# Retention followed by a GELU MLP on one core: block 5's first product by seven half-size products, some differences of g on GpSimd, masks one by one, loads in another order

## The chip, the cores and the metric

The kernel runs on one core of a Trainium2 chip. The metric is the device time of one execution in microseconds (us). Three runs of the kernel before gave 300.93 us as their median (300.79 to 301.58). The engines are called as in the profile: PE (matrix products, with PEld for the weight loads beside it), DVE (vector), ACT (scalar), POOL (GpSimd, which also issues most of the loads), SP (which issues the loads of v and the stores).

## What is computed

```python
scores = scale * q @ k.T                      # 8 batches, 8 heads, 576 positions, 64 per head
ret    = scores * Dmat                        # gamma[h] ** (row - col) where row >= col, else 0
x      = (ret @ v), heads side by side        # 4608 tokens x 512
h      = x @ w_in                             # 512 -> 2048, "first product"
g      = 0.5 * h * (1 + erf(h / sqrt(2)))     # GELU
out    = g @ w_out                            # 2048 -> 512, "second product"
```

Inputs and output are float32; the kernel works in bfloat16 with float32 sums.

## The kernel before

The retention is done in chunks of 128 positions with a running state, so that a chunk needs its own scores and the state of the chunk ahead of it. A unit is one chunk of one batch (the last chunk of 64 positions joins two batches); a group is the same chunk of two batches. There are 36 units in 22 groups. For each group q and k are loaded and turned (by PE for groups 0 to 7, `turn`, and by a DVE transpose from group 8 on, `turn_dve`), the scores are made (`scores`, tile `sc`), multiplied by a mask into `ret` (`masked`, on DVE), multiplied by the scaled values `vh` (`scaled_v`, DVE or POOL) and joined with the state (`inner`, `cross`, tile `o_ps`); `evacuate` scales the result into a tile of x on DVE. `state` makes the next state from k, v (tile `u_ps`).

Four units make a block of 512 tokens, and there are nine blocks, 0 to 8. The first product of a block is by default 16 steps of four 128x512 matmuls (`mlp1`, tile `hT`), each followed by a GELU on ACT into `g_all`. In the blocks of `FAST1` (6, 7, 8) it is Winograd's form of Strassen's method instead: the product is cut into 2x2 parts and seven half-size products do for eight (`mlp1_fast`, 4 runs of 7 steps, each step four 128x256 matmuls, tiles `ha` and `hb`). It needs sums of the parts of w_in, made once (`w_in_sums`), sums of the parts of x (`x_sum`, four for each block), three copies of `ha` out of PSUM in each run (`either`: DVE or ACT, whichever the planner sees free first) and three additions on DVE (`plus`). The steps run in the order 1, 2, 6, 5, 7, 4, 3. The second product is `mlp2` (tile `oT`) or, in the blocks of `FAST2` (1 to 8), the same seven-product form in two halves of 256 tokens (`mlp2_fast`, 7 steps of eight 128x256 matmuls, tiles `fa` and `fb`); each half needs four sums or differences of g (`g_sum`, 128x1024 bfloat16, both inputs in SBUF, called s1 to s4 here; the third overwrites a part of g itself).

The order of everything is decided while the program is built: a planner keeps an expected clock for each engine (`T`), appends the next step whose inputs it expects to be ready, and gives idle DVE time to side jobs (`side_jobs`, chosen by a priority). On the chip each engine then runs its own list in that order and waits on semaphores alone. An engine that has nothing ahead in its list starts an instruction as soon as the semaphores allow, whatever clock the planner had in mind. Loads by POOL stand in its list in the order of `ORDER`, extended by `reload`; at most eight of them are under way. The eight PSUM banks are shared by all of this.

Of the kernel before, what the change touches and what calls it, by code (L numbers as in the profile page):

```python
# [17 lines left out]
def kernel(  # L18
# [47 lines left out]
    FAST1 = (6, 7, 8)  # L66
# [3 lines left out]
    N_LD = 4  # L70
    N_QKT = 4
    N_KN = 4
    VH_POOL = 20
    N_VH = 6
    N_XB = 4
    ALLOW = 0
    AHEAD = 14
    RATE = 3.8
    HOT = 7.5
    SLACK, SB, PER_G, PER_B, TURN0 = 1.6, 9.0, 8.0, 40.0, 3.0  # L80
# [5 lines left out]
    V_LEAD = 4  # L86
# [46 lines left out]
    near = ld_pool.tile([128, 2, HP, 128], FP32, tag="qk", bufs=N_LD, name="near")  # L133
# [77 lines left out]

    sw = [0.0]
# [16 lines left out]
    def qk_tile(name):  # L229
        return ld_pool.tile([128, 4 * H * D], BF16, tag="qk", bufs=N_LD, name=name)  # L230
# [4 lines left out]
    def tiles_of(i):  # L235
        g = groups[group_of[i]]
        if i not in loaded:
# [3 lines left out]
            else:  # L241
                n = group_of[i]
                if i != g[0]:
                    qk, kn = loaded[i - 1][0], loaded[i - 1][2]
                elif n not in BY_DVE:
                    qk = qk_tile("qk_ld").rearrange("p (a h j d) -> p a h j d", a=2, h=H, j=2)
                    kn = qk[:, 1]
                else:
                    qk = qk_tile("qkb_ld").rearrange("p (a f) -> p a f", a=2)
                    kn = ld_pool.tile([128, H, 2, D], BF16, tag="kn", bufs=N_KN, name="kn_ld") if len(g) > 1 else None  # L250
                loaded[i] = (qk, None if group_of[i] in BY_DVE else ld_pool.tile([128, H, D], BF16, tag="v", bufs=8, name="v_ld"), kn)
# [13 lines left out]
    def load(what, i):  # L265
# [43 lines left out]
        for jj in (j,) if j is not None else range(2):  # L309
# [3 lines left out]
            else:  # L313
# [7 lines left out]
    ORDER = ("wi0 io v0 k1 q1 v1 wi1 q2 k2 v2 wi2 k3 q3 v3 wi3 wi4 wi5 wi6 wi7 wo0 wo1 wo2 wo3 wo4 wo5 wo6 wo7 "  # L321
             "q4 k4 q5 k5 v4 v5 dq2 q6 k6 q7 k7 v6 v7 q8 k8 q9 k9 v8 v9 dq3 q10 k10 v10 dq4 q11 k11 q12 k12 n11 n12 dq0").split()
# [9 lines left out]

    def reload():
        if next_load[0] < N_G:
            g = groups[next_load[0]]
            if next_load[0] not in BY_DVE:
                ORDER.extend(f"{what}{i}" for what in "qkv" for i in g)
            else:
                ORDER.extend([f"{what}{i}" for what in "qk" for i in g] + [f"n{i}" for i in g if len(g) > 1])
            next_load[0] += 1  # L340

# [50 lines left out]
    def qkT_of(n):  # L392
        s = sg[n]
        if "qkT" not in s:
            if n < 4:
                s["qkT"] = ld_pool.tile([128, 2, HP, 128], BF16, tag="kn", bufs=N_KN, name="qkT")
            else:
                s["qkT"] = tr_pool.tile([128, 2, H, 128], BF16, tag="qkT", bufs=N_QKT, name="qkT")
# [88 lines left out]

    def masked(i):
        s = st[i]
        if i not in raw and any(x[3] is make_msk for x in later):  # L490
            finish_later()
        (got, done) = s.pop("sc")
        s["ret"] = []
        short = units[i][2] is None
        if short:
            r = ret_pool.tile([128, H, TAIL], BF16, tag="ret0", name="ret0")
        for e in range(2):
            b, t = got[e]
            sl = slice(64 * e, 64 * e + 64)
            if short and group_of[i] in BY_DVE:  # L500
                nc.vector.tensor_tensor(r[:, HP * e:HP * e + HP, :], t, msk2.to_broadcast([128, HP, TAIL]), op=ALU.mult)
            elif short:
                nc.vector.tensor_tensor(r[sl], t[sl], msk[sl, :, sl].to_broadcast([64, H, TAIL]), op=ALU.mult)
            else:
                r = ret_pool.tile([128, HP, 128], BF16, tag=f"ret{e}", name=f"ret{e}")
                by = near[:, e] if i in raw else (mskp if group_of[i] in BY_DVE else msk).to_broadcast([128, HP, 128])
                nc.vector.tensor_tensor(r, t, by, op=ALU.mult)  # L507
            s["R"] = on("dve", 0.42 if short and group_of[i] in BY_DVE else 0.66, done) + SEM
            release(b, s["R"])
            s["ret"].append(r)  # L510
# [209 lines left out]
    def g_sum(t, p, i):  # L720
# [7 lines left out]
        nc.vector.tensor_tensor(s[i], x, y, op=op)  # L728
        s["at" + i] = on("dve", 0.66, max(g_at[t, m, ts] for m in range(N_DF) for ts in (2 * p, 2 * p + 1))) + SEM
# [92 lines left out]
    def w_in_sums():  # L822
        def make(i, h):
            def go():
                if i not in ws:
                    ws[i] = qk_tile("ws" + i)[:, 0:HC * HF].rearrange("p (c f) -> p c f", c=HC)
# [9 lines left out]
    def x_sum(t, i):  # L836
# [4 lines left out]
        s[i] = ld_pool.tile([128, HC, HT], BF16, tag="v", bufs=8, name="x" + i)  # L841
# [5 lines left out]
    fast1 = {}  # L847

    def mlp1_fast(t, i, name):
# [31 lines left out]
        if name in "167":  # L881
            key = {"1": "t1", "6": "t2", "7": "t3"}[name]
            if key != "t2":
                f["tt"] = tr_pool.tile([128, 2, 2, HT], FP32, tag="qkT", bufs=N_QKT, name="tt")
            f[key] = f["tt"][:, key == "t2"]
# [17 lines left out]
    def fast1_ready(t, i, name):  # L903
        f, s = fast1.get((t, i), {}), xs.get(t, {})
        if ("f", t - 2, 0, "3") in waiting2 or nT < N_G or name == "7" and ("f", t - 2, 1, "4") in waiting2:
            return 1e9
        k_ = 2 * i + (name == "7")
        if name in "17" and t == FAST1[0] and k_ < N_QKT and nB <= groups[N_G - N_QKT + k_][-1]:
# [20 lines left out]
    for t in range(N_BLK):  # L929
# [13 lines left out]
        elif t == 0:  # L943
            runs2.append((t, [("2", t, ts, m, m + 2) for m in range(0, N_DF, 2) for ts in range(2)]))
            runs2.append((t, [("2", t, ts, m, m + 4) for ts in range(2, 4) for m in range(0, N_DF, 4)]))
# [36 lines left out]
    nA = nB = nT = nV = 0  # L982
# [7 lines left out]
    def xsum_ready(t, i):  # L990
        if t > FAST1[0] + 1 and ("h", t - 2, 3, {"1": "5", "2": "6", "4": "4", "3": "7"}[i]) in waiting2 or nV < N_U:
# [4 lines left out]
    for t in FAST2:  # L996
        for p in range(2):
# [5 lines left out]
    def sum_ready(t, p, i):  # L1003
        if i != "3" and t > FAST2[0] and not done_step(t - 1, p, {"1": "5", "2": "6", "4": "3"}[i]):
# [228 lines left out]
```

## Time and profile before

| what | value | from |
|---|---|---|
| median of three runs | 300.93 us | times |
| the profiled execution, whole | 300.81 us | times |
| its span, first to last instruction | 298.9 us | profile page |
| PE busy | 286.1 us, 96% | profile page |
| DVE busy | 226.7 us, 76% | profile page |
| ACT busy | 135.1 us, 45% | profile page |
| POOL busy | 152.9 us, 51%, nothing after 181.3 us | profile page |
| granted TensorE clock | 0.996 | times |

Busy counts any overlap once, and matmuls are pipelined: eight 128x256 matmuls that follow each other without a gap take 0.87 us, although one of them is shown with 273 ns. DVE instructions overlap in the same way at their ends: four masks in a row take 2.45 to 2.48 us, 0.60 us from one start to the next, although each is shown with about 0.68 us. Sums over the body are therefore made with the distance from start to start. In the trace block 1's first product begins at 51.7 us, that of block 5 at 175.3, block 6 at 208.8, block 7 at 230.7 and block 8 at 255.1 us.

### The profile page before, as it was taken

To read this page: it belongs to the slowest core of one execution; us is meant where nothing else is said; L and a number is where in the kernel's file an instruction comes from. 1 tells how busy PE (TensorE), PEld (TensorE's weight loads), DVE (VectorE), ACT (ScalarE), POOL (GpSimd) and SP (SyncE) were. 2 spreads that over 40 slices of the span, in tenths; PEclk is the share of its full clock that TensorE was granted. 3 is DMA by queue.
4 is the path that set the end of the run, shared out by engine and by line. 5 is a ranking of instruction groups with operands and counts; after the bars stand their busy time and mean duration, and the time that the engine had idled before them with its cause. 6 is when DMAs were issued, how large, how long until landed. Compare 5 with 4: busy or idle time off the path is not lost.

```text
span 298.9 us, 8793 instructions
## 1 busy us (share of the span) xinstructions
PE 286.1 (96%) x3689; PEld 213.8 (72%) x3718; DVE 226.7 (76%) x432; ACT 135.1 (45%) x262; POOL 152.9 (51%) x232
## 2 busy tenths in 40 slices
PE   7899997999999999999998999999999999999994
PEld 2478555888657656667665666666888888888883
DVE  5762059999999889317969489756998999898751
ACT  7656225744343343542542434433554554546421
POOL 8976797899896899996986842000000000000000
PEclk9999999999999999999999999999999999999998
DMA  9999999999999999999979570201001101111014
GB/s 143 166 186 204 182 187 179 214 163 113 155 141 197 189 201 125 155 162 159 139 126 174 83 188 2 72 2 37 35 2 72 71 2 70 44 28 72 35 55 124
DMA packets 112119, 34.79 MB, mean 116 GB/s; under 512 B 89808, under 2 KB 107728, under 8 KB 112080
## 3 DMA queue, kind: packets, MB, share of 16 engines
q0 software_dynamic: 78048, 17.71, 66.8%
q1 hardware_dynamic: 32992, 16.26, 20.2%
q8 instruction: 29, 0.48, 0.7%
q10 hardware_dynamic: 1040, 0.26, 0.4%
q14 instruction: 10, 0.08, 0.1%
HBM read 42.47 MB, written 9.44 MB: 174 GB/s over the span
## 4 chain that ended last, share of the span: by engine, by line
PE 62%; DMA 16%; POOL 16%; issue 3%; DVE 1%; ACT 0%; POOLq 0%; DVEq 0%; ACTq 0%
PE fa L760 17%; PE hT L656 14%; PE fb L760 13%; PE ha L865 7%; PE hb L865 5%; POOL qkb_ld L298 5%; DMA qkb_ld<-in_q_dram 3%; DMA qk_ld<-in_q_dram 3%; POOL kn_ld L305 3%; DMA kn_ld<-in_k_dram 3%; DMA w_out<-in_moe_w_out_dram 3%; POOL early L315 3%; DMA qk_ld<-in_k_dram 3%; PE sc L462 2%; POOL w_in L270 2%
## 5 line engine op out<-in xcount | busy, mean ns | idle before, releaser
L656 PE MATMUL hT<-x,w_in 128*128 128x512 bf16 (+2 forms) x521 | 92.6, 314 | 3.1 <-DVE x L636 1.0
L656 PEld LDWEIGHTS <-w_in 128*128 128x128 bf16 x544 | 49.1, 98 | 26.1 <-issue 3.2
L661 ACT ACTIVATE g_all<-hT 128x512 bf16<-128x512 f32 x64 | 38.2, 597 | 49.8 <-PE hT L656 47.6
L760 PEld LDWEIGHTS <-g_all 128*128 128x128 bf16 x512 | 49.6, 98 | 11.0 <-issue 0.2
L760 PEld LDWEIGHTS <-s 128*128 128x128 bf16 x384 | 37.4, 98 | 8.9 <-issue 0.2
L746 DVE TENSOR_TENSOR o_sb<-fb,t 128x256 f32<-128x256 f32 x48 | 19.9, 417 | 25.4 <-ACT t L375 12.9
L870 ACT ACTIVATE g_all<-tt 128x512 bf16<-128x512 f32 x36 | 22.6, 630 | 29.4 <-DVE tt L878 29.3
L298 POOL DMA_DIRECT2D qkb_ld<-in_k_dram x56 | 30.9, 587 | 6.5 <-DMA kn_ld<-in_k_dram 4.7
L760 PE MATMUL fa<-w_out,g_all 128*128 128x256 bf16 x256 | 33.1, 273 | 0.0
L305 POOL DMA_DIRECT2D kn_ld<-in_k_dram x44 | 30.4, 731 | 5.2 <-PE u_ps L557 2.3
L298 POOL DMA_DIRECT2D qkb_ld<-in_q_dram x56 | 31.3, 599 | 2.2 <-DMA qkb_ld<-in_k_dram 1.2
L507 DVE TENSOR_TENSOR ret<-sc,mskp 128x512 bf16<-128x512 f32 x44 | 27.2, 677 | 3.2 <-PE sc L462 3.1
L878 DVE TENSOR_TENSOR tt<-hb,tt 128x512 f32<-128x512 f32 x36 | 24.5, 687 | 5.2 <-ACT tt L375 2.9
L664 ACT ACTIVATE g_all<-hT 128x512 bf16<-128x512 f32 (+1 forms) x36 | 19.2, 550 | 14.2 <-PE hT L656 14.1
L375 ACT COPY t<-fa 128x256 f32<-128x256 f32 x35 | 13.0, 371 | 19.6 <-PE fa L760 19.6
L636 DVE TENSOR_TENSOR x<-o_ps,dqT 128x512 bf16<-128x512 f32 (+1 forms) x36 | 20.9, 619 | 0.8 <-PE o_ps L613 0.6
L865 PEld LDWEIGHTS <-ws 128*128 128x128 bf16 x192 | 18.8, 98 | 2.2
L516 POOL TENSOR_TENSOR vh<-v,dvp 128x512 bf16<-128x512 f32 x14 | 15.1, 1134 | 5.2 <-DMA v<-in_v_dram 5.2
L430 DVE STREAM_TRANSPOSE qkT<-qkb_ld 128x512 f32<-128x512 f32 (+1 forms) x28 | 17.4, 637 | 0.0
L760 PE MATMUL fb<-w_out,g_all 128*128 128x256 bf16 x128 | 16.6, 273 | 0.0
L760 PE MATMUL fb<-w_out,s 128*128 128x256 bf16 x128 | 16.4, 273 | 0.1
L760 PE MATMUL fa<-wt,g_all 128*128 128x256 bf16 x128 | 16.4, 273 | 0.0
(123 smaller groups left out, 445.2 us busy)
## 6 DMA issues: line engine op xcount, KB each, us to landing
out_dram<-o_sb SPq DMA_DIRECT2D x31, 256.0 KB, 2.8
v<-in_v_dram SPq DMA_DIRECT2D x50, 128.0 KB, 4.7
qkb_ld<-in_q_dram POOLq DMA_DIRECT2D x44, 64.0 KB, 3.6
qkb_ld<-in_k_dram POOLq DMA_DIRECT2D x44, 64.0 KB, 3.8
kn_ld<-in_k_dram POOLq DMA_DIRECT2D x44, 64.0 KB, 4.5
w_in<-in_moe_w_in_dram POOLq DMA_DIRECT2D x8, 256.0 KB, 7.1
w_out<-in_moe_w_out_dram POOLq DMA_DIRECT2D x8, 256.0 KB, 9.8
out_dram<-o_sb SPq DMA_DIRECT2D x8, 128.0 KB, 2.4
```

What stands on the lines that cost most here:

```text
L298: nc.gpsimd.dma_start(qk[p0:p0 + 32, "qk".index(what), 0:HP * per].rearrange("p (h x) -> p h x", h=HP), {"q": q, "k": k}[what][2 * bp + jj ...
L305: nc.gpsimd.dma_start(kn[64 * e:64 * e + 64, :, j], k[2 * bp + j, :, ci * C + e:ci * C + C:2, :].rearrange("h s d -> s h d"))
L507: nc.vector.tensor_tensor(r, t, by, op=ALU.mult)
L636: nc.vector.tensor_tensor(x[:, :, n * y:n * y + n], o, dqT[:, :, ci * C:ci * C + n], op=ALU.mult)
L656: nc.tensor.matmul(hT[:, m - m0, :], lhsT=w_in[:, cc, m * 128:m * 128 + 128], rhs=x_tiles[t][:, cc, lo:hi], start=(cc == 0), stop=(cc == N ...
L661: nc.scalar.activation(g_all[:, t % 2, :, m0, :], hT.rearrange("p n (a c) -> p (n a) c", a=2), AF.Gelu)
L664: nc.scalar.activation(g_of(t, 2 * lo // TOK)[:, m0:m0 + n, lo_:lo_ + hi - lo], hT, AF.Gelu)
L746: nc.vector.tensor_tensor(dst, src, f[key], op=ALU.add)
L760: nc.tensor.matmul(dst, lhsT=x[:, kk, :], rhs=y[:, kk, :], start=(name in "125" and kk == 0), stop=(kk == HK - 1), skip_group_check=True)
L865: nc.tensor.matmul(dst[:, m, :], lhsT=a[:, cc, c0:c0 + 128], rhs=y[:, cc, :], start=(name in "125" and m == 0 and cc == 0), stop=(cc == HC ...
L870: nc.scalar.activation(g_of(t, part)[:, m0:m0 + 2], src, AF.Gelu)
L878: nc.vector.tensor_tensor(f[key], f["b"][1], f[key], op=ALU.add)
```

## The change

- `FAST1` gets block 5: its 16 steps of `mlp1` become 4 runs of seven steps of `mlp1_fast`, which may now stand among the last attention groups (`fast1_ready`). One of the sums of w_in is written over w_in itself (`ws["3"]`), one gets its own tile.
- The second half of block 0's second product becomes the seven-product form as well, with its own four sums of g.
- Masks: `masked` only lists them, and `mask` makes one at a time as a side job.
- `g_sum` may be put on POOL when POOL is expected to be idle after 130 us of the planner's clock and the sum is not due at once. Of the 68 sums of the changed program 16 stand on POOL: s1 to s4 of the second half of blocks 4, 5 and 7, s1 to s3 of the second half of block 6, s1 of the second half of block 8. The other 52 stand on DVE (64 before).
- The loads: `ORDER` is another permutation, and from group 9 on a group's loads are listed only when the group whose buffer they take has been turned; the buffers of loads, turned tiles and values are split or reduced (`qk` 4 to 2 + 2, `kn` 4 to 3, `v` 8 to 7, `vh` 6 to 5).
- The planner's weights change.

```diff
-    FAST1 = (6, 7, 8)
+    FAST1 = (5, 6, 7, 8)
+    G_LD = 16
+    G_QKT = 16
-    N_LD = 4
-    N_QKT = 4
-    N_KN = 4
-    VH_POOL = 20
-    N_VH = 6
+    N_KN = 3
+    VH_POOL = 22
+    N_VH = 5
-    AHEAD = 14
-    RATE = 3.8
+    AHEAD = 12
+    RATE = 5.1
+    GP_FROM, GP_LEFT = 130.0, 2.0
+    MSLACK, MASK0 = 1.6, 0.0
+    STATE10 = 24.0
-    SLACK, SB, PER_G, PER_B, TURN0 = 1.6, 9.0, 8.0, 40.0, 3.0
+    SLACK, SB, PER_G, PER_B, TURN0 = 1.6, 4.0, 6.0, 30.0, 3.0
-    V_LEAD = 4
+    V_LEAD = 2
...
+        return ld_pool.tile([128, 4 * H * D], BF16, tag="qk" if n >= G_LD or n % 2 == 0 else "qk_b", bufs=2, name=name)
...
-    ORDER = ("wi0 io v0 k1 q1 v1 wi1 q2 k2 v2 wi2 k3 q3 v3 wi3 wi4 wi5 wi6 wi7 wo0 wo1 wo2 wo3 wo4 wo5 wo6 wo7 "
-             "q4 k4 q5 k5 v4 v5 dq2 q6 k6 q7 k7 v6 v7 q8 k8 q9 k9 v8 v9 dq3 q10 k10 v10 dq4 q11 k11 q12 k12 n11 n12 dq0").split()
+    ORDER = ("wi0 io k2 v0 q1 k1 q2 k3 v1 wi1 q3 v2 wi2 wi5 wi4 wi3 k4 v3 wo2 wi7 wo0 wi6 wo1 wo3 wo6 wo4 wo5 wo7 "
+             "q5 q4 k5 v4 v5 k6 k7 q6 q7 q8 k9 q9 v7 v8 k8 dq2 dq3 v6 dq4 q10 q11 v9 q12 k10 v10 dq0 k12 k11").split()
...
     def masked(i):
+        s = st[i]
+        s["ret"], s["R"] = [], 1e9
+        mask_due.extend((i, e) for e in range(2))
+
+    def mask(i, e):
...
-    def g_sum(t, p, i):
+    def g_sum(t, p, i, by_pool=False):
...
-        nc.vector.tensor_tensor(s[i], x, y, op=op)
-        s["at" + i] = on("dve", 0.66, max(g_at[t, m, ts] for m in range(N_DF) for ts in (2 * p, 2 * p + 1))) + SEM
+        after = s.get("at" + {"2": "1", "4": "2"}.get(i, ""), 0.0)
+        (nc.gpsimd if by_pool else nc.vector).tensor_tensor(s[i], x, y, op=op)
+        s["at" + i] = on(*(("pool", 2.2) if by_pool else ("dve", 0.66)), max(after, *(g_at[t, m, ts] for m in range(N_DF) for ts in (2 * p, 2 * p + 1)))) + SEM
...
-                    ws[i] = qk_tile("ws" + i)[:, 0:HC * HF].rearrange("p (c f) -> p c f", c=HC)
+                    if i == "3":
+                        ws[i] = w_in[:, 0:HC, HF:]
+                    elif i == "4":
+                        ws[i] = const.tile([128, HC, HF], BF16, name="ws4")
+                    else:
+                        ws[i] = ld_pool.tile([128, HC, HF], BF16, tag="qk_b", bufs=2, name="ws" + i)
...
-            runs2.append((t, [("2", t, ts, m, m + 4) for ts in range(2, 4) for m in range(0, N_DF, 4)]))
+            runs2.append((t, [("f", t, 1, x) for x in "1265743"]))
...
-    for t in FAST2:
-        for p in range(2):
+    for t in (0, *FAST2):
+        for p in range(2) if t else (1,):
             sum_due += [(t, p, i) for i in "1234"]
...
+        if mask_due and (T["dve"] <= now + MSLACK or T["pe"] < 30):
+            jobs.append(((group_of[mask_due[0][0]] - gB) * PER_G + MASK0, lambda: mask(*mask_due.pop(0))))
+        if sum_due and T["pool"] <= now + 0.3 and now > GP_FROM and sum_ready(*sum_due[0]) <= now + 0.1:
+            t, p, i = sum_due[0]
+            if (t + 0.5 * p - b2) * 25.0 > GP_LEFT:
+                jobs.append((99.0, lambda: g_sum(*sum_due.pop(0), True)))
...
-        if u_due and state_at(*u_due[0]) <= T["pe"] + 0.2 and not (u_due[0] == (1, 0) and nA < 6):
+        if u_due and state_at(*u_due[0]) <= T["pe"] + 0.2 and not (u_due[0] == (1, 0) and T["pe"] <= STATE10):
```

In the changed program's lists, block 5's seven-product steps stand between attention groups 18 and 21; the first state of the second pair of batches (`state(1, 0)`) stands among block 0's first product instead of behind it; the eight sums of w_out and the four sums of g for block 0 stand on DVE ahead of the turning of group 4.

## The prediction

> **What bounds the kernel now.** I read the busy time by stretch first, then the chain of work, then the timelines of PE and DVE where PE stops. Columns of the first: stretch, length, then PE, PEld, DVE, ACT, POOL busy (instructions), clock, DMA.
>
> ```profile
> 40.00:60.00 20.00, 18.11 (x314) 13.13 (x315) 19.07 (x32) 10.27 (x21) 16.81 (x25) 1.00 2.08 199
> ...
> 220.00:240.00 20.00, 20.00 (x186) 17.93 (x184) 18.36 (x37) 10.17 (x19) 0.00 (x0) 1.00 0.15 54
> 240.00:260.00 20.00, 20.00 (x186) 17.93 (x184) 18.04 (x34) 10.95 (x20) 0.00 (x0) 1.00 0.11 40
> ```
>
> From 20 us on PE hardly stops; in the last third it never does, and DVE runs beside it at 90%. So PE's work and PE's stops set the time. The chain gives PE's pace (start, length, step):
>
> ```profile
> 191.23 1.73 PE hT L656 x8
> ...
> 261.40 0.87 PE ha L865 x8
> ...
> 276.24 0.87 PE fa L760 x8
> ```
>
> A 128x512 matmul takes 1.73/8 = 0.216 us, a 128x256 one 0.87/8 = 0.109. PE's largest stop in the body lies at 40 to 52 us (PE, then DVE):
>
> ```profile
> 47.54 0.41 PE L542 MATMUL o_ps<-ret,vh 128*64 128x128 bf16 x8 [0.60 <-DVE vh L516]
> ...
> 51.74 1.03 PE L656 MATMUL hT<-x,w_in 128*128 128x256 bf16 x8 [0.81 <-DVE x L636]
> ```
> ```profile
> 39.74 1.09 DVE L373 COPY qkT<-qk_ps 128x512 bf16<-128x512 bf16 x3 [15.05 <-PE qk_ps L407]
> ...
> 44.77 2.71 DVE L516 TENSOR_TENSOR vh<-v_ld,dv 128x512 bf16<-128x512 bf16 x2
> ```
>
> DVE was idle for 15.05 us and then could not keep up; block 1's first product waits for x. That vh pair took 2.71 us where two cost 1.28. The reason shows where POOL computes (DVE, then POOL):
>
> ```profile
> 145.59 0.68 DVE L728 TENSOR_TENSOR g_all<-g_all 128x1024 bf16<-128x1024 bf16 x1
> ...
> 148.88 1.34 DVE L728 TENSOR_TENSOR s<-g_all 128x1024 bf16<-128x1024 bf16 x1
> 150.26 1.43 DVE L728 TENSOR_TENSOR s<-s,g_all 128x1024 bf16<-128x1024 bf16 x1
> ```
> ```profile
> 147.12 2.55 POOL L516 TENSOR_TENSOR vh<-v,dvp 128x512 bf16<-128x512 f32 x2
> 149.64 1.49 POOL L516 TENSOR_TENSOR vh<-v,dv 128x512 bf16<-128x512 f32 x1
> ```
> ```profile
> 180.38 1.47 DVE L728 TENSOR_TENSOR s<-g_all 128x1024 bf16<-128x1024 bf16 x1
> ```
> ```profile
> 180.24 1.06 POOL L516 TENSOR_TENSOR vh<-v,dv 128x512 bf16<-128x512 f32 x1
> ```
>
> A DVE sum with both inputs in SBUF (0.68 us) that meets a POOL operation of that kind does not start until POOL ends: 180.38 + 1.47 = 181.85, POOL's end at 181.30 plus 0.55. At 148.88 to 151.7 they alternate: POOL's two end at 149.67, DVE ends 0.55 later, POOL's third 0.9 after that, DVE 0.56 later. DVE operations with one input in PSUM, and transposes, beside POOL's are not longer.
>
> **The change part by part.** The profiled execution took 300.81 us (1.9 outside its span), 0.12 under the median; the sum starts from 300.8.
>
> *Block 5's first product.* 64 x 0.216 = 13.8 us of PE go; 4 runs x 7 steps x 4 x 0.109 = 12.2 come: -1.6. DVE gets 12 additions (0.60 each), 12 copies that DVE and ACT share, and four sums of x (0.34). The eight sums of w_in only move earlier.
>
> *Block 0's second half.* 32 x 0.216 = 6.9 go, 56 x 0.109 = 6.1 come: -0.8.
>
> *The stop at 40 to 52 us.* The eight sums of w_out (0.60 each, now between 47 and 57 us) and the copy for the first state move into DVE's idle 15 us: 5.4 us less in the queue ahead of block 1; block 0's second half puts back three joins of 0.33. The walk: the second product of block 0 starts about 31; its first half ends near 38, when q and k of groups 4 and 5 land as before; scores of group 4 at 41, four masks and two vh by 45.2, attention at 45.5, block 1's first step at 48.4 instead of 51.7 with one step of 0.87 left over. That is 2.4 to 2.9 earlier, 0.8 of it counted: -1.9. Ends: 0 (the loads decide) and -2.9.
>
> *Loads reordered.* wi1 moves behind three more strided loads (0.87 us each by their distance on POOL): the first product starts about 14.3 instead of 11.8, but group 2's turning and scores run there. wi6 is the last needed; by landings of 1.3 us for each weight piece at about 28, with 1.8 us of PE work behind it, so 31.5 stands: 0 (ends -0.9, +2). Fewer buffers from group 16 on: eight issues of 0.59 and 3.6 to landing are 8.3 us, groups come every 10 to 16: 0 (ends 0, +2). vh of units 34 and 35 now stand behind two POOL sums of 2.0; their attention comes 15 us later: 0. SP's loads and stores move by less than their slack: 0.
>
> *Masks one by one.* The same 72 instructions. They free their PSUM bank singly; the two stops at scores (0.6 at 106.5, 1.2 at 161.8) may shrink: -0.7 (0 to -1.8).
>
> *Sums on POOL.* No trace shows a 128x1024 sum on POOL. 128x256 takes 0.625, 128x512 1.06: two steps of 0.435 more give 1.93; twice vh's usual mean of 1.13 gives 2.27. I take 2.0, near the first, which is the undisturbed one. [...]
>
> The gain is 12 fewer sums on DVE. The loss is where they stand. POOL has nothing else then, so s1 starts once the block's last GELU ends, not when the planner meant; s2, s3, s4 follow at once. In just that time DVE makes the sums of the first half and of x. Each can wait for a whole POOL sum, and everything behind it on DVE (copies of ha that PE needs before it may add to the bank) waits too. [...]
>
> Block 6, from the end of its last step: GELU ends at 1.5, POOL's s1 runs 1.8 to 3.8. DVE wants the second sum of x at 2.3: it waits to 3.8, ends 4.2. POOL's s2 to 6.2; the third sum of x waits and ends at 6.6. Then an addition and the copy of ha: 7.8. PE wanted that copy at 5.2: 2.6 lost. Afterwards s3 delays nothing that PE is close to.
> Block 5: s2 of the first half waits 2.0 (PE loses 0.9, and 0.3 at a copy behind it), s3 waits 1.0 for POOL's s4 (0.8): 2.0.
> Block 7: s2 waits 1.7 (1.3), s3 1.4 (0.8): 2.1.
> Block 8: s2 of the first half waits, and the second half's s2, on DVE, needs POOL's s1: 1.1.
> Block 4: DVE is full there (about 27 us of work in 29 of PE), four sums meet vh and s1 to s4; 0 to 4, as the masks' slack is unknown; I take 1.0, nearer the low end, because the sum at 180.38 waited for a vh in the same stage and PE did not stop.
> Sum +8.8. Ends: 0, if the spare tenth of DVE takes all, and 12.
>
> *Sum:* -1.6 - 0.8 - 1.9 - 0.7 + 8.8 = +3.8: 304.6 us.
>
> **The rivals.**
> (a) The other side: DVE's spare time takes up the waits. From 220 to 280 us DVE is busy for 18 of 20 us and the POOL sums take 12 x 0.60 off it, so 3 to 5 us in each block are free. Against it: PE needs a copy within about 1 us, and the waits come in clusters. It decides below 5.0 us in all, 0.3 for each of 16 sums. Without waits: 300.8 - 5.0 = 295.8; with 1 us of them 296.8.
> (b) Waits as forecast, and the front fails: block 0's first product starts 2.5 us later and the loads do not make it good. For it: until 52 us PE waits on landings. 304.6 + 1.9 + 2.0 = 308.5.
> (c) The change does not do what it says: in block 5 DVE (27 of 29 us) becomes the bound, so that the 1.6 do not come, and the waits cost about as much as the front gains: 300.8.
> (d) Block 4 at its upper end, 4.0 instead of 1.0: 307.6.
>
> **How the numbers follow.** Forecast 0.40, (a) 0.38, (b) 0.06, (c) 0.08, (d) 0.08. About 0.3%, 0.9 us, is what a measurement here tells from no change. Slower: forecast, (b), (d): 0.54, of which 0.02 may end within the bound; same (c) with that, 0.08 + 0.02; faster (a), 0.38, less 0.02 that ends within the bound too. So 0.36, 0.12, 0.52. The range reaches from (a) with the stop at 40 to 52 us gone to its end of -2.9 (295.8 - 1.0 = 294.8) to (d), 307.6. The forecast's own, with the waits from three quarters (6.6) to POOL sums of 2.27 (10.0): 302.4 to 305.8.
>
> **What would show it.** Right: sums on POOL of 1.9 to 2.3 us that start within 1 us of a block's last GELU, DVE sums of x or g of 1.5 to 2.6 us beside them, and stops of PE of 1 to 3 us behind DVE copies (L390) in blocks 5 to 7, with PE below 19 of 20 us there. Block 1's first product at 48 to 49 us, block 6's first step some 5 us earlier than 208.8, the lead then lost. Wrong: DVE's sums at 0.68 beside POOL's; PE still at 20 of 20 there; or a front that is late.

## The result and the profile after

The changed kernel takes 318.95 us (median; 317.5 to 321.09) against 300.86 us for the kernel before: a ratio of 1.0587, with an interval of 1.0546 to 1.0628. It is slower by far more than the 3.8 us of the forecast. The profiled execution took 321.09 us, 319.3 of them its span, with a mean granted clock of 0.976 where it was 0.996. Times and ratios below leave out the one execution that came in a slow state (318.79 us, in the run with POOL sums cut in quarters).

The busy time by stretch of the changed kernel, with the columns as in the prediction (the last three are clock, DMA share and GB/s):

```profile
40.00:60.00 20.00, 18.62 (x297) 15.62 (x294) 17.67 (x33) 9.08 (x18) 18.59 (x24) 1.00 1.83 175
...
140.00:160.00 20.00, 16.66 (x368) 11.04 (x368) 19.38 (x28) 4.40 (x9) 12.13 (x18) 0.91 0.89 147
...
180.00:200.00 20.00, 15.52 (x263) 12.15 (x256) 19.86 (x24) 4.90 (x10) 13.14 (x8) 0.83 0.15 39
...
220.00:240.00 20.00, 18.14 (x163) 15.53 (x162) 18.75 (x32) 8.60 (x16) 9.22 (x4) 1.00 0.07 27
240.00:260.00 20.00, 16.89 (x142) 14.32 (x140) 17.79 (x28) 7.84 (x14) 6.56 (x3) 0.91 0.07 27
```

Before, PE filled 20.00 of the 20 us in the last two of these. Now PE stops at least once in each of blocks 4 to 8, and in three of these stretches the granted clock is below 1.00. Three places carry most of the loss.

**Block 6.** What the prediction walked through is here nearly step for step. POOL makes s1 and s2 of block 6's second half as soon as the last GELU has ended, and two DVE sums of x (0.41 us each where nothing meets them) take 4.48 us together. POOL's timeline, then DVE's, then PE's (start, length, instruction, and in brackets the idle time ahead with what ended it):

```profile
247.25 2.12 POOL L753 TENSOR_TENSOR s<-g_all 128x1024 bf16<-128x1024 bf16 x1 [16.42 <-ACT g_all L901]
249.45 2.18 POOL L753 TENSOR_TENSOR s<-s,g_all 128x1024 bf16<-128x1024 bf16 x1
```
```profile
247.43 4.48 DVE L874 TENSOR_TENSOR x<-x,x 128x512 bf16<-128x512 bf16 x2
251.83 0.68 DVE L909 TENSOR_TENSOR tt<-hb,tt 128x512 f32<-128x512 f32 x1
252.43 0.67 DVE L390 COPY tt<-ha 128x512 f32<-128x512 f32 x1
```
```profile
249.44 0.60 PE L896 MATMUL ha<-x,w_in 128*128 128x256 bf16 x4
253.16 1.01 PE L896 MATMUL ha<-x,w_in 128*128 128x256 bf16 x4 [3.12 <-DVE tt L390]
253.97 1.06 PE L896 MATMUL hb<-x,w_in 128*128 128x256 bf16 x4
254.82 1.79 PE L785 MATMUL fa<-w_out,g_all 128*128 128x256 bf16 x8
```

The last two lines show something that is not in the prediction. A step of four takes 0.81 to 0.85 us from start to start behind the stop, where it takes 0.44, and one of eight 1.62 instead of 0.87. PE works at half pace for about 3.3 us, 1.5 of them lost on top of the stop.

**Block 4.** The same, and worse. The two in-place sums of w_in (L861) stand in DVE's list at 178.89, ahead of a join of the state on which PE's next step waits. POOL has four vh, s1 and s2 in a row there:

```profile
176.86 4.21 POOL L540 TENSOR_TENSOR vh<-v,dvp 128x512 bf16<-128x512 f32 x4
180.93 2.21 POOL L753 TENSOR_TENSOR s<-g_all 128x1024 bf16<-128x1024 bf16 x1
183.22 2.46 POOL L753 TENSOR_TENSOR s<-s,g_all 128x1024 bf16<-128x1024 bf16 x1
```
```profile
178.89 7.33 DVE L861 TENSOR_TENSOR w_in<-w_in 128x1024 bf16<-128x1024 bf16 x2
186.14 0.68 DVE L596 TENSOR_TENSOR u_acc<-u_ps,u_acc 128x512 f32<-128x512 f32 x1
```
```profile
181.78 0.61 PE L896 MATMUL ha<-x,w_in 128*128 128x256 bf16 x4
186.87 1.87 PE L785 MATMUL fa<-w_out,g_all 128*128 128x256 bf16 x8 [4.48 <-DVE u_acc L596]
188.53 1.06 PE L896 MATMUL hb<-x,w_in 128*128 128x256 bf16 x4
```

The pair takes 7.33 us instead of 1.28 and ends 0.54 us after s2 does. PE stops for 4.5 us, and its next four steps lose another 2.2 us to half pace (0.8, 0.4, 0.4 and 0.6).

**148 to 158 us.** This has no POOL sum in it at all. POOL stands from 139.1 to 144.1, until a load buffer is free, with the scaled values behind the loads in its list. (The row names a mask, L523, just behind the transpose that empties the buffer; with four buffers, below, POOL does not stand.)

```profile
144.13 2.20 POOL L303 DMA_DIRECT2D qkb_ld<-in_q_dram  x4 [5.01 <-DVE ret L523]
...
153.22 3.09 POOL L540 TENSOR_TENSOR vh<-v,dvp 128x512 bf16<-128x512 f32 x3
```
```profile
153.34 0.32 PE L556 MATMUL o_ps<-ret,vh 64*64 64x64 bf16 x16 [2.91 <-POOL vh L540]
```
```profile
151.42 5.44 DVE L753 TENSOR_TENSOR s<-g_all 128x1024 bf16<-128x1024 bf16 x1
```

PE waits for a vh, and meanwhile a DVE sum of 0.69 us waits until four vh in a row have ended (156.31). It stood from 151.42, 0.78 us before the first of them began, while POOL was still issuing loads; what held it then the rows do not show.

The front did come earlier: block 1's first product begins at 49.95 instead of 51.74, that of block 3 at 108.53 instead of 110.47. The lead is gone after the stops at 150 and 182 us: block 6's first step, which the prediction had some 5 us earlier than 208.8, comes at about 218.

### The profile page after: what moved, and what is told of

It is laid out like the page before. It is cut to its first block, busy times and chain, and to the rows that moved or that the text cites. A ratio compares the mean times of both kernels' runs of the same rounds, so it can differ in the third digit from the quotient of the medians.

```text
span 319.3 us, 9043 instructions
## 1 busy us (share of the span) xinstructions
PE 292.1 (91%) x3794; PEld 222.8 (70%) x3815; DVE 260.3 (82%) x463; ACT 133.0 (42%) x257; POOL 188.5 (59%) x246
## 5 line engine op out<-in xcount | busy, mean ns | idle before, releaser
L680 PE MATMUL hT<-x,w_in 128*128 128x256 bf16 (+2 forms) x485 | 76.8, 300 | 1.3 <-DMA w_in<-in_moe_w_in_dram 0.3
L785 PEld LDWEIGHTS <-g_all 128*128 128x128 bf16 x544 | 53.3, 100 | 17.8 <-issue 5.1
L753 POOL TENSOR_TENSOR s<-g_all 128x1024 bf16<-128x1024 bf16 x5 | 11.0, 2205 | 83.1 <-ACT g_all L901 83.1
L680 PEld LDWEIGHTS <-w_in 128*128 128x128 bf16 x504 | 43.6, 98 | 18.7 <-issue 1.0
L901 ACT ACTIVATE g_all<-tt 128x512 bf16<-128x512 f32 x48 | 30.1, 630 | 48.7 <-DVE tt L909 48.5
L685 ACT ACTIVATE g_all<-hT 128x512 bf16<-128x512 f32 x48 | 28.5, 597 | 38.3 <-PE hT L680 37.7
L909 DVE TENSOR_TENSOR tt<-hb,tt 128x512 f32<-128x512 f32 x48 | 32.7, 685 | 8.9 <-ACT tt L392 6.3
L896 PE MATMUL ha<-x,w_in 128*128 128x256 bf16 x192 | 27.8, 275 | 3.3 <-DVE tt L390 3.1
L896 PEld LDWEIGHTS <-w_in 128*128 128x128 bf16 x256 | 25.2, 100 | 7.6 <-issue 3.8
L390 DVE COPY tt<-ha 128x512 f32<-128x512 f32 x31 | 20.9, 678 | 0.0
L785 PE MATMUL fa<-wt,s 128*128 128x256 bf16 x136 | 17.7, 273 | 3.2 <-DVE s L753 3.2
```

Source lines behind the costliest of these rows:

```text
L390: nc.vector.tensor_copy(dst, src)
L680: nc.tensor.matmul(hT[:, m - m0, :], lhsT=w_in[:, cc, m * 128:m * 128 + 128], rhs=x_tiles[t][:, cc, lo:hi], start=(cc == 0), stop=(cc == N ...
L685: nc.scalar.activation(g_all[:, t % 2, :, m0, :], hT.rearrange("p n (a c) -> p (n a) c", a=2), AF.Gelu)
L785: nc.tensor.matmul(dst, lhsT=x[:, kk, :], rhs=y[:, kk, :], start=(name in "125" and kk == 0), stop=(kk == HK - 1), skip_group_check=True)
L896: nc.tensor.matmul(dst[:, m, :], lhsT=a[:, cc, c0:c0 + 128], rhs=y[:, cc, :], start=(name in "125" and m == 0 and cc == 0), stop=(cc == HC ...
L901: nc.scalar.activation(g_of(t, part)[:, m0:m0 + 2], src, AF.Gelu)
```

## The experiments

The theory at this point: the POOL sums hold DVE off, PE stops behind DVE, and behind a long stop PE is slow for a while. The rivals: DVE is simply full with block 5 in seven products, or the front and the buffers cost the time. The table has all runs, each as its ratio to the kernel before, which ran beside it. Differences between runs are given below as the difference of two ratios times 300.4 us (about the median of the kernel before in these runs), with the root of the sum of the squares of both intervals' halves. A trace is of one execution. Those of the run with block 5 plain and of the one with four vh on DVE are about 2 us faster than the median of their run, those of four buffers and of the quarters 2 and 3 us slower.

| run | median, us | ratio | interval |
|---|---|---|---|
| the changed kernel | 318.95 | 1.0587 | 1.0546 to 1.0628 |
| its sums of g all on DVE | 305.35 | 1.0124 | 1.0069 to 1.0180 |
| POOL only writes in place of its sums | 303.05 | 1.0081 | 1.0049 to 1.0112 |
| before, with the 16 sums on POOL | 320.78 | 1.0684 | 1.0638 to 1.0730 |
| changed, block 5 in plain steps | 313.17 | 1.0445 | 1.0382 to 1.0507 |
| both undone | 302.64 | 1.0060 | 1.0025 to 1.0095 |
| idle matmuls in two stops | 319.84 | 1.0625 | 1.0554 to 1.0697 |
| sums on DVE, four vh on DVE | 304.37 | 1.0128 | 1.0067 to 1.0190 |
| both undone, four buffers of q and k | 302.13 | 1.0044 | 1.0010 to 1.0078 |
| front and masks alone | 298.36 | 0.9942 | 0.9918 to 0.9967 |
| block 0 alone, loads as before | 301.91 | 1.0049 | 1.0023 to 1.0075 |
| front and masks with the new weights | 298.70 | 0.9937 | 0.9913 to 0.9961 |
| POOL sums cut in quarters | 314.39 | 1.0479 | 1.0424 to 1.0533 |

### All sums of g on DVE

```diff
-    GP_FROM, GP_LEFT = 130.0, 2.0
+    GP_FROM, GP_LEFT = 1e9, 2.0
```

> The changed kernel with all 68 sums of g on DVE; everything else of the change stays, and the planner orders its list anew. Theory (the POOL sums hold DVE off, and PE stops behind that and slows down after it): PE's losses at 224, 249 to 255, 282 to 287 and 305 us go (2.4 + 3.1 + 1.5 + 2.1 + 1.0 = 10.1 us), and of the 6.7 at 182 to 192 us at least half, since vh alone is left on POOL there; the stop at 149 to 153 us (2.9 + 1.8), which comes from a late vh, may stay. 318.95 less 10 to 16: 303 to 309 us, and no DVE sum over 1.5 us after 192 us. Rival (DVE, at 82%, is simply full with block 5 in seven products; the place of the sums matters little): 16 sums of 0.60 more on DVE, 314 to 325 us, with PE still waiting for DVE copies in blocks 5 to 7.

305.35 us, in the middle of the theory's range: 13.9 us (11.8 to 16.0) less than the changed kernel. After 192 us one stop over 0.4 us is left (0.52 at 221, for a DVE copy in block 6). DVE does all 68 sums, and PE hardly waits for it in blocks 6 to 8. DVE was not full there; the place of the sums was the loss.

### POOL writes the same tiles and reads nothing

```diff
-        (nc.gpsimd if by_pool else nc.vector).tensor_tensor(s[i], x, y, op=op)
+        if by_pool:
+            nc.gpsimd.memset(s[i], 0.0)
+        else:
+            nc.vector.tensor_tensor(s[i], x, y, op=op)
```

> The changed kernel in the same order, but where POOL makes one of its 16 sums it only fills the tile with zeros: same tiles, same semaphores, no input read. It leaves out these 16 sums, so its time is that of the same program with POOL writing alone. Theory (what holds DVE off is that POOL reads and writes SBUF for the whole instruction): if the reading is what counts, the 15 us of extra DVE time beside these sums go and only that beside vh stays (4.8 at 151 us, 2 to 4 at 179 us); 318.95 less 10 to 14: 305 to 309 us. Rival 1 (any POOL instruction of that length holds DVE off): DVE's sums wait for the fill as for a sum, and the time follows the length of a fill. Rival 2 (PE waits for the results of POOL, not for DVE): the time stays with the fill's length, 316 to 319 us if a fill takes 2 us.

303.05 us, 15.2 us (13.6 to 16.8) less than the changed kernel with the same order on every engine; the theory had said 305 to 309 if the reading is what counts. In the trace, the waits beside vh are still there, those beside the 16 places are gone: the pair of sums of w_in in block 4 takes 3.06 us, held by vh alone (until 179.60), where it took 7.33. One meeting, POOL and then DVE:

```profile
238.62 0.95 POOL L754 MEMSET g_all<- 128x1024 bf16 x1 [4.83 <-ACT g_all L904]
```
```profile
238.81 0.87 DVE L877 TENSOR_TENSOR x<-x,x 128x512 bf16<-128x512 bf16 x2
```

Two sums of x start inside the fill and take 0.41 and 0.42 us, as without it. A fill takes 0.95 to 1.07 us instead of 2.12 to 2.6 and, as it needs no input, often runs at another time, so few meetings are left: five DVE sums touch a fill, four of them begin inside one, and none is longer for it. So the run shows that what POOL does in these 16 places costs 15 us; that it is the reading, and not the length, rests on these few meetings.

### The kernel before with the 16 sums on POOL

```diff
-        nc.vector.tensor_tensor(s[i], x, y, op=op)
+        on_pool = p == 1 and (t in (4, 5, 7) or t == 6 and i != "4" or t == 8 and i == "1")
+        (nc.gpsimd if on_pool else nc.vector).tensor_tensor(s[i], x, y, op=op)
```

> The kernel before with nothing changed but the engine of these 16 sums (s1 to s4 of the second half of blocks 4, 5 and 7, s1 to s3 of block 6, s1 of block 8): POOL instead of DVE, the order of every list kept. Theory (the POOL sums are the loss): the waits come in blocks 6 to 8 as in the changed kernel, 2.4 + 4.6 + 2.1 + 1.0 us, and somewhat less in block 4, where DVE has no block 5 to serve: 300.9 plus 7 to 14, 308 to 315 us. Rival (DVE's spare time takes them up when the planner has not moved other work): 297 to 302 us.

320.78 us, 20.5 us slower than before: this one edit costs as much as the whole change, and more than the theory's 7 to 14. One of its largest stops is at the sums of w_in, which the old list has in block 6 (DVE, POOL, PE):

```profile
214.71 5.13 DVE L832 TENSOR_TENSOR ws<-w_in 128x1024 bf16<-128x1024 bf16 x2
```
```profile
214.33 2.44 POOL L729 TENSOR_TENSOR s<-g_all 128x1024 bf16<-128x1024 bf16 x1 [22.11 <-ACT g_all L661]
216.85 2.44 POOL L729 TENSOR_TENSOR s<-s,g_all 128x1024 bf16<-128x1024 bf16 x1
```
```profile
221.09 0.60 PE L866 MATMUL ha<-x,ws 128*128 128x256 bf16 x4 [3.10 <-DVE tt L373]
```

PE's stops of 0.8 us and more from 190 us on add up to 13.6 us (2.2, 3.1, 2.9, 1.3, 3.2, 0.9), and the granted clock is 0.91, 0.91, 0.83 and 0.91 in four stretches of 20 us behind them. So the sums on POOL alone bring a loss of this size with the old list too.

### Block 5 in plain steps

```diff
-    FAST1 = (5, 6, 7, 8)
+    FAST1 = (6, 7, 8)
```

> The changed kernel with block 5's first product in 16 plain steps again; the POOL sums stay, the planner orders anew. Theory: this gives back 1.6 us of matmuls, but the additions, copies and in-place sums of w_in that stood behind vh, s1 and s2 at 179 to 187 us are no longer due there, so the 4.5 us stop and the half pace behind it (2.2) go; the stops in blocks 6 to 8 (10 us) stay: 318.95 + 1.6 - 4 to 6.7, 314 to 317 us. Rival (block 5 in seven products makes DVE the bound all through 144 to 210 us, and the POOL sums matter little): 303 to 309 us. Rival 2 (the stop comes from elsewhere): 319 to 322 us.

313.17 us, 4.3 us (2.0 to 6.5) less than the changed kernel, and just under the theory's range. The stop of 4.5 us at 182 is gone, with one of 1.7 at 187 us (waiting for masks) in its place. In the list planned anew the stops in blocks 5 to 8 stay too, but they are smaller than the 10 us that the theory kept: 2.1 us at 220, 1.0 at 246, 0.8 at 252 and 0.7 at 298.

### Both undone

```diff
-    FAST1 = (5, 6, 7, 8)
+    FAST1 = (6, 7, 8)
-    GP_FROM, GP_LEFT = 130.0, 2.0
+    GP_FROM, GP_LEFT = 1e9, 2.0
```

> The changed kernel with block 5's first product in 16 plain steps and all sums of g on DVE, so that only the front, the masks, the buffers and the planner's weights are left of the change. Together with the run of the changed kernel (318.95), with the sums on DVE alone undone (305.35) and with block 5 alone undone (313.17) it makes a table of two by two. Theory (block 5's loss is the meeting of its sums of w_in with vh and the POOL sums, so the two parts interact; without POOL sums block 5's form costs about nothing): 305 to 307 us, that is 305.35 plus at most the 1.6 us of matmuls. Rival (block 5 has a loss of its own, so the two add up): 305.35 - 5.8 = 299.6 us, 298 to 301.

302.64 us, between the two: neither the 305 to 307 of the theory nor the 299.6 of the rival. Without POOL sums block 5's seven products cost 1.9 us (-0.1 to 3.9), with them 4.3. The interaction of 2.3 us has an interval of 3 on either side, so it stays open; what is shown is that the 1.6 us of matmuls bring no gain in either case. A reason that the trace offers, and that no run isolates: with block 5 in seven products and the sums on DVE, DVE has no spare time there (its column is the fourth number):

```profile
180.00:200.00 20.00, 18.91 (x235) 16.25 (x234) 19.76 (x35) 8.69 (x17) 2.38 (x2) 1.00 0.15 37
200.00:220.00 20.00, 19.57 (x291) 16.19 (x290) 19.65 (x37) 9.31 (x17) 0.00 (x0) 1.00 0.08 28
```

### Idle matmuls in the stops

```diff
+    def fill(n):
+        b = frees(1)[0]
+        t = ps.tile([128, 512], FP32, tag=b, name="fill")
+        for _ in range(n):
+            nc.tensor.matmul(t, lhsT=w_out[:, 0, :128], rhs=w_out[:, 0, :], start=True, stop=True)
...
+            if pick[2][0] in (("h", 7, 0, "7"), ("f", 4, 0, "1")):
+                fill(12 if pick[2][0][0] == "h" else 16)
```

> The changed kernel with nothing moved but idle matmuls ahead of the two steps behind which PE went at half pace (16 of 128x512 ahead of the step that waited 4.48 us at 182 us, 12 ahead of the one that waited 3.12 us at 249 us, 0.216 us each, into a free bank that nothing reads). Theory (after a stop of about 3 us the granted clock falls, whatever caused the stop, and the half pace behind it costs 2.25 and 1.5 us): the waits stay, the half pace behind the two goes, the granted clock at 180 to 200 us is 1.00 instead of 0.83 and at 240 to 260 us 1.00 instead of 0.91; 318.95 - 3.8: 314 to 316 us. Rival (the slow pace is PE waiting in small pieces for DVE, which the records do not show as waits): the pace stays, 318 to 321 us.

The time did not move (319.84 us, the rival's), but the two places differ. At 182 us the fill missed: its bank was freed by DVE, so the idle matmuls waited 4.92 us with everything else and then took 5.86 us of PE's time. At 250 us it landed in the stop (PE, then DVE, then the stretch):

```profile
250.56 2.75 PE L1133 MATMUL fill<-w_out 128*128 128x512 bf16 x12
253.85 0.60 PE L896 MATMUL ha<-x,w_in 128*128 128x256 bf16 x4 [0.54 <-DVE tt L390]
254.28 0.60 PE L896 MATMUL hb<-x,w_in 128*128 128x256 bf16 x4
254.72 1.04 PE L785 MATMUL fa<-w_out,g_all 128*128 128x256 bf16 x8
```
```profile
248.11 4.49 DVE L874 TENSOR_TENSOR x<-x,x 128x512 bf16<-128x512 bf16 x2
```
```profile
240.00:260.00 20.00, 19.46 (x168) 16.15 (x166) 17.77 (x29) 8.34 (x16) 6.57 (x3) 1.00 0.07 27
```

DVE waits as before (4.49 us), the same PE step starts as late as before, but it and the next ones go at 0.43 and 0.44 us, and the granted clock is 1.00 instead of 0.91. From block 7's first step to block 8's it is 27.33 us instead of 28.83: 1.5 us, as expected. So here the half pace is the clock's answer to PE standing still, and not a hidden wait.

### Four scaled values on DVE

This starts from the run with all sums on DVE.

```diff
-        on_pool = i >= VH_POOL
+        on_pool = i >= VH_POOL and i not in (26, 27, 28, 29)
```

> The kernel with all sums of g on DVE (305.35), and in it the scaled values of units 26 to 29 on DVE instead of POOL. Theory (the stop at 148 to 150 us comes from these four values: they stand on POOL behind the loads for which POOL had waited 5.9 us, and then hold a DVE sum for 4.64 us): the stop of 2.1 us, the half pace behind it (some 1.7) and the 4 us of DVE waiting go, DVE has 4 x 0.64 = 2.6 us more work; 305.35 - 2 to 4: 301 to 303.5 us, granted clock 1.00 at 140 to 160 us. Rival (the loads behind POOL's wait are late in themselves, and PE stops for them some us later): 304.5 to 307 us.

304.37 us, just under the rival's range and above the theory's: by the ratios 0.1 us from the run it starts from, with an interval of 2.5 on either side. What happens is what the rival says. The stop at 148 us and the slow clock behind it are gone (PE 20.00 of 20 at 140 to 160), and 13 us later there is another of at least that size, since POOL still stands for a buffer (4.28 us, to 153.84) and its loads are late:

```profile
162.02 0.41 PE L566 MATMUL o_ps<-ret,vh 128*64 128x128 bf16 x8 [0.75 <-POOL vh L540]
165.15 0.19 PE L581 MATMUL u_ps<-vh,kn_ld 128*32 128x64 bf16 x1 [2.71 <-DMA kn_ld<-in_k_dram]
```

### Four buffers of q and k again

This starts from the run with both undone; `tag` is the rotation from which a buffer is taken.

```diff
-        tag="qk" if n >= G_LD or n % 2 == 0 else "qk_b"
+        tag="qk" if n % 2 == 0 else "qk_b"
...
-        if wsum1 and nT >= G_LD and ...
+        if wsum1 and nT >= N_G and ...
```

> As the run with both parts undone, and the load buffers of q and k from group 16 on again four in rotation instead of two (the sums of w_in then come after the last group). POOL's list is the same in both. Theory (the loss at 140 to 160 us comes from POOL standing until a buffer is free, with the scaled values behind it): POOL's wait of about 6 us ahead of the loads at 142 us shrinks below 2, the stop at 148 us and the half pace behind it go; 3 to 4 us less than the run with both undone, about 302 us, or 296 to 299 if that run is at 299.6. Rival (the 12 loads ahead of the values take 7 us to issue in any case): within 1 us of the run with both undone.

302.13 us, within 0.5 us of the run with both undone, as the rival had it. POOL's list is the same in both, and POOL no longer stands. The first line is POOL with both undone, the second POOL with four buffers:

```profile
141.64 2.20 POOL L303 DMA_DIRECT2D qkb_ld<-in_q_dram  x4 [5.77 <-DVE qkT L447]
```
```profile
136.65 2.19 POOL L303 DMA_DIRECT2D qkb_ld<-in_q_dram  x4
```

But PE stops at 148 us all the same, 1.28 us for a DVE sum that has now met the earlier vh (4.17 us long), and 1.47 us for masks behind it. The wait on the buffer was not the cause by itself. What stays the same is the order of POOL's list: one group's loads, then four scaled values.

### Front and masks alone, then with the new weights

The changed kernel with `FAST1`, the sums of g, the buffers of loads and values and the weights of before; the second run puts the new weights back.

```diff
-    FAST1 = (5, 6, 7, 8)
-    N_KN = 3
-    VH_POOL = 22
-    N_VH = 5
-    AHEAD = 12
-    RATE = 5.1
-    GP_FROM, GP_LEFT = 130.0, 2.0
-    SLACK, SB, PER_G, PER_B, TURN0 = 1.6, 4.0, 6.0, 30.0, 3.0
-    V_LEAD = 2
+    FAST1 = (6, 7, 8)
+    N_KN = 4
+    VH_POOL = 20
+    N_VH = 6
+    AHEAD = 14
+    RATE = 3.8
+    GP_FROM, GP_LEFT = 1e9, 2.0
+    SLACK, SB, PER_G, PER_B, TURN0 = 1.6, 9.0, 8.0, 40.0, 3.0
+    V_LEAD = 4
```

(Also eight buffers of v and four of q and k in rotation, with the sums of w_in in these after the last group, and the loads of groups 17 to 21 listed one or two groups earlier, as the buffers allow. The turned tiles stay as in the changed kernel.)

> What is left of the changed kernel when block 5, the sums of g, the buffers (q and k four in rotation, kn 4, v 8, vh 6, first value on POOL unit 20) and the planner's weights are those of the kernel before: the order of the first loads, block 0's second half in seven products with its sums early, the masks one by one. Theory (these three are worth what the prediction said, -0.8, -1.9 and -0.7, and the run with both parts undone, at 302.64, loses it to the stops at 148 to 156 and 184 to 188 us that come with fewer buffers): 300.4 - 2 to 3.4: 297 to 298.5 us, no stop of 1.5 us after 60 us. Rival (the front's lead is lost behind it whatever the buffers, since the loads of the later groups do not come earlier): 300 to 302 us.

> The run with front and masks (298.36), with the planner's weights of the changed kernel (AHEAD 12, RATE 5.1, the priorities 4, 6, 30, V_LEAD 2) and still the buffers of the kernel before. Between it and the run with both parts undone (302.64) only the buffers are left. Theory (fewer buffers cost the 4.3 us between the two): 297.5 to 299.5 us, PE at 19 of 20 us or more at 140 to 160 us. Rival (the weights cost them, as they order the attention groups later and closer together): 301 to 303.5 us, with stops of 1.5 us or more at 140 to 160 us.

298.36 and 298.70 us, both in their theory's range, and 0.9942 and 0.9937 of the kernel before: both beat both kernels, the first the kernel before by 1.7 us (1.0 to 2.5). With the old buffers PE has no stop over 0.8 us after 60 us, whatever the weights. Between the second run and the one with both undone the buffers of kn, v, vh and q and k differ, and with them when the last groups' loads are listed and from which unit on the values are on POOL: 3.7 us (2.4 to 5.0). The two buffers of q and k alone were not it. Which of the others it is was not tried. POOL's list is another too: in the second run three scaled values (144.97 to 148.09) stand ahead of loads that come at 148.00, where the run with both undone has those loads first, at 141.64 behind a wait of 5.77 us, and then four values.

### Block 0 alone

The kernel before, with these edits (and the first state of the second pair of batches after 24 us):

```diff
-            runs2.append((t, [("2", t, ts, m, m + 4) for ts in range(2, 4) for m in range(0, N_DF, 4)]))
+            runs2.append((t, [("f", t, 1, x) for x in "1265743"]))
...
-    for t in FAST2:
-        for p in range(2):
+    for t in (0, *FAST2):
+        for p in range(2) if t else (1,):
...
-            jobs.append(((FAST2[0] - b2) * PER_B, lambda: wsum.pop(0)[1]()))
+            jobs.append(((0.5 - b2) * PER_B, lambda: wsum.pop(0)[1]()))
```

> The kernel before with only block 0's second half in seven products, its sums of w_out ahead of the turning of group 4 and the first state of the second pair of batches among block 0's steps; loads, masks, buffers and weights as before. Theory: the stop at 48 to 52 us shrinks and block 1's first product begins 2 us earlier than 51.7; 300.4 - 0.8 - 1.0 to 1.9: 297.7 to 298.6 us. Rival (PE waits for the landings of groups 4 and 5 there, so that earlier sums change nothing, and half a microsecond of the 0.8 goes to three joins on DVE): 299.6 to 300.8 us.

301.91 us, slower than before by 1.5 us (0.7 to 2.3) and outside both ranges. Block 1's first product begins at 51.67 us, as before (51.74). With the loads in the new order, in all runs that have it, it begins at 49.8 to 50.5. So the earlier front needs the new order of the loads (or the single masks, which this run lacks too, or both), and block 0's form without them is a loss.

### POOL sums in quarters

```diff
-        (nc.gpsimd if by_pool else nc.vector).tensor_tensor(s[i], x, y, op=op)
+        for c in ([slice(k, k + 2) for k in range(0, HK, 2)] if by_pool else [slice(0, HK)]):
+            (nc.gpsimd if by_pool else nc.vector).tensor_tensor(s[i][:, c], x[:, c], y[:, c], op=op)
```

> The changed kernel in the same order, each of its 16 POOL sums cut into four pieces of 128x256 that follow each other and do not depend on each other (0.6 us each, so about 2.5 us for a sum instead of 2.12). Theory (POOL instructions that follow each other without a wait do not let DVE in, so that only the whole of them counts): a DVE sum that meets them still waits for all four, 1.5 to 2.3 us over its 0.69, and the time is 319 to 325 us. Rival (the two take turns, as the prediction assumed): a DVE sum waits for one piece, 0.6 us at most, and the time falls to 306 to 313 us.

314.39 us, between the two ranges and 3.2 us (1.2 to 5.3) less than the changed kernel. In blocks 5 to 8 the engines take turns by the piece: a DVE sum of g that meets them there takes 0.75 to 1.18 us instead of up to 2.5, and PE has no stop over 0.4 us after 193 us. In block 4 the opposite is seen (POOL, then two DVE sums of this run, then PE):

```profile
182.89 2.54 POOL L754 TENSOR_TENSOR s<-s,g_all 128x256 bf16<-128x256 bf16 x4
185.39 1.05 POOL L540 TENSOR_TENSOR vh<-v,dvp 128x512 bf16<-128x512 f32 x1
186.41 1.05 POOL L540 TENSOR_TENSOR vh<-v,dv 128x512 bf16<-128x512 f32 x1
187.42 2.53 POOL L754 TENSOR_TENSOR g_all<-g_all 128x256 bf16<-128x256 bf16 x4
189.92 2.98 POOL L754 TENSOR_TENSOR s<-g_all,s 128x256 bf16<-128x256 bf16 x4
```
```profile
183.49 8.27 DVE L754 TENSOR_TENSOR s<-g_all 128x1024 bf16<-128x1024 bf16 x1
...
226.99 1.09 DVE L754 TENSOR_TENSOR s<-g_all 128x1024 bf16<-128x1024 bf16 x1
```
```profile
192.41 1.01 PE L897 MATMUL hb<-x,ws 128*128 128x256 bf16 x4 [7.21 <-DVE ret L529]
```

One DVE sum stood for 8.27 us while eleven more POOL instructions passed, each starting as the one ahead ended. PE then waited 7.21 us for masks behind that sum, and the clock was at half from 187.5 to 197.7 us. The sum at 226.99 got in behind a single piece. So neither the theory nor the rival holds throughout.

## Why the prediction came out so

The direction and the main cause were right: the sums on POOL hold DVE off, PE stops behind DVE's copies and sums, and rival (a), in which DVE's spare time takes the waits up, is out (the sums on DVE again give 13.9 us back). The size was wrong by a factor of almost five, and for several reasons. By the terms, with the steps between the runs above:

| step of the prediction | forecast, us | measured, us |
|---|---|---|
| block 0's second half, the stop at 40 to 52 us, the loads' order, masks | -0.8 - 1.9 + 0 - 0.7 | -1.7 (-2.5 to -1.0) together |
| the planner's weights | 0 | -0.2 (-1.2 to 0.9) |
| fewer buffers | 0 (ends 0, +2) | +3.7 (2.4 to 5.0) |
| block 5's first product | -1.6 | +1.9 (-0.1 to 3.9) |
| sums on POOL | +8.8 (ends 0, 12) | +13.9 (11.8 to 16.0) |
| sum | +3.8 | +17.6 |

- **Sums on POOL, blocks 5 to 8: right.** The walks gave 2.0, 2.6, 2.1 and 1.1 us. By the distances from step to step in the profile after PE lost 2.4, 3.3, 2.1 and 1.0, behind the DVE sums that the walks named. POOL's sum takes 2.12 us undisturbed and up to 2.6 beside DVE, for 2.0 with bounds of 1.93 and 2.27. That all 16 sums hold DVE off as a vh did was the author's estimate, from the meetings in the profile before (1.47 us for a sum of 0.68); the profile after shows two sums of x, of 0.41 us each, that take 4.48 together.
- **Sums on POOL, block 4: the step that failed most.** "I take 1.0, nearer the low end" of 0 to 4: it was a stop of 4.65 us from step to step, over the upper end, and 2.2 us of half pace, so 6.9 in place of 1.0. The row that it was taken from (the sum at 180.38 that met a vh, with PE running on) was a single meeting that cost DVE 0.8 us. After the change two sums of w_in stand at that place, and POOL's work there is four vh and two sums in a row. (The trace's losses at POOL sums, 8.8, 6.9 and 1.5 of half pace in block 6, add up to 17.2 us and not 13.9: the profiled execution took 2.1 us more than the median, and the run without these sums has a stop of its own of 1.1 us at 183.)
- **A cost with no term.** Behind each of the three longest stops (3.12, 4.48 and 2.91 us) the granted clock was 0.50 for a while: 1.5 us lost in block 6, 2.2 in block 4, about 1.7 at 153 us. The idle matmuls show the cause in block 6 (1.00 instead of 0.91 at 240 to 260 us). The profile before had no stop over 1.0 us in the body, and the walks ended when PE could start, not when it was back at pace.
- **"DVE and POOL alternate": only sometimes so.** At 148.88 in the profile before they did, and in blocks 5 to 8 they do. In the profile after a DVE sum waits for four vh from 151.42 on, and in the quarters' run for eleven instructions.
- **"Fewer buffers from group 16 on: 0": wrong**, and above the upper end. "Eight issues of 0.59 and 3.6 to landing are 8.3 us, groups come every 10 to 16" has the time for the loads themselves, but not POOL's list: behind a load that waits for its buffer (5.01 us in the profile after) stand the scaled values. Two runs that took away one part of it moved the stop or left it; it went only with all the old buffers together, which also gives POOL another list. Which of these is the cause stays open.
- **Block 5: the gain of 1.6 did not come.** Rival (c) had said so, and its reason (DVE full) is what the stretches of the run with the sums on DVE show; no run isolates it.
- **The front: -1.8 us at block 1's first product, for 3.3 forecast** ("48.4 instead of 51.7"; it was 49.95). The prediction gave the gain to the sums that move into DVE's idle time. The run with block 0 alone shows that these, with the loads and masks as before, leave the first product where it was. The walk had q and k of groups 4 and 5 landing as before, near 38 us; in the profile after PE still waits 1.19 us for a landing of q at 45.81. Rival (b), a front that fails, did not happen.

## What to carry to other kernels

An operation that is moved to an idle engine is to be priced by what it meets there: here 16 sums of 2 us, off the path and on an engine with nothing to do, cost 14 us, and one pair of DVE sums ahead of a PE step (7.33 us for 1.28) was enough to turn a meeting into a stop of 4.48 us. A stop of PE is to be priced with the half pace that may follow it: here 1.5 to 2.2 us more behind stops of 2.91 to 4.48 us. Before a buffer is taken away, read what else stands in the list of the engine that issues its loads.

## What the runs showed of the hardware

**A held-off DVE instruction does not always get the next turn.** Within one run the same kind of DVE sum got in behind one POOL instruction (1.09 us) or stood until eleven more had passed (8.27 us); in the profile after it was four (5.44 us). POOL's instructions followed each other without a gap in all of these. What decides was not found. Beside POOL's issuing of loads of kn a DVE sum was longer in one place and not in another: in the profile before a sum of g at 146.53 took 1.21 us for 0.68 (POOL issued such loads until 147.21 and had a vh from 147.12 on), and in the profile after one at 164.67 took 0.68.

**Of two stops of about the same length, one was followed by half pace.** In the run with block 5 plain, a stop of 1.89 us is followed by a granted clock of 0.50, and one of 2.13 us by 1.00. First PE's rows, then the busy time by stretch (columns as above; the clock is the third number from the right):

```profile
150.95 0.32 PE L556 MATMUL o_ps<-ret,vh 64*64 64x64 bf16 x16 [1.89 <-POOL vh L540]
...
221.83 1.05 PE L785 MATMUL fa<-wt,s 128*128 128x256 bf16 x8 [2.13 <-DVE s L753]
```
```profile
148.75:152.16 3.41, 1.52 (x54) 0.87 (x53) 3.41 (x4) 0.44 (x2) 3.41 (x5) 1.00 1.25 82
152.16:155.57 3.41, 3.41 (x31) 2.05 (x29) 3.41 (x6) 0.60 (x1) 2.22 (x2) 0.50 0.71 161
...
217.01:220.43 3.42, 2.69 (x25) 2.15 (x23) 3.23 (x6) 1.86 (x4) 3.34 (x2) 1.00 0.00 0
220.43:223.84 3.41, 2.01 (x19) 1.81 (x20) 3.15 (x4) 0.86 (x2) 0.79 (x1) 1.00 0.00 0
223.84:227.25 3.41, 3.41 (x34) 3.06 (x32) 3.21 (x6) 1.84 (x4) 0.00 (x0) 1.00 0.00 0
```

In the profile after all times at which the granted clock falls or rises lie whole multiples of 3.413 us apart: it is at half from 153.95 to 157.36, 184.67 to 191.49, 252.93 to 256.35 and from 317.79 to the end. If a run's time is cut into windows of 3.413 us that end there, the first of the two stops lies in one window, in which PE is busy for 1.52 us, and the next window goes at half pace. The second is split into 0.73 and 1.40 us, and neither window is answered. From 25 us on, in the profiles before and after, the clock was at half behind six such windows, in which PE stood for 2.19 to 2.88 us, and behind none in which it stood for 1.58 or less. That where a stop falls decides is the author's reading of these rows, and no run moved a stop across such a border. One window with 1.89, in the run with idle matmuls (147.48 to 150.89), was not answered: the granted clock is 1.00 from 140 to 160 us there. What else counts is open.
